# Top-k attention and a low-rank mixer in one kernel: weighted values moved from the middle of a step to the head of the next one

## The chip, the cores and the metric

The kernel runs on one core of a Trainium2 chip. A core has a matrix engine (TensorE, PE in the profile), a vector engine (VectorE, DVE), a scalar engine (ScalarE, ACT), a general-purpose engine (GpSimd, POOL) and a queue that issues transfers (SyncE, SP). Each works through its own queue in order; they wait for each other by semaphores. The time is the device time of the core in microseconds, the median over runs; beside it stands one execution that was recorded instruction by instruction.

## The reference, cut to what matters

Two blocks follow each other. Attention keeps only the 32 largest scores of each row:

```python
# q, k, v: (8, 8, 576, 64)
scores = scale * np.matmul(q, k.transpose(0, 1, 3, 2))
kth = np.partition(scores, -top_k, axis=-1)[..., -top_k:-top_k + 1]
scores = np.where(scores >= kth, scores, -1000000000.0)
attn = np.exp(scores - np.max(scores, axis=-1, keepdims=True))
attn = attn / (np.sum(attn, axis=-1, keepdims=True) + 1e-09)
attn_out = np.matmul(attn, v)
```

The heads are then laid side by side, x of shape (8, 576, 512), and a mixer runs over them:

```python
h = x.transpose(0, 2, 1) @ U @ V          # U: (576, 32), V: (32, 576)
u = x + h.transpose(0, 2, 1)
out = u + np.maximum(u @ w_ch1, 0.0) @ w_ch2   # 512 -> 2048 -> 512
```

## The kernel before, in words

**Tiles and steps.** A pair of heads of one batch is a unit of work `g`; there are 32 (four per batch, `NPAIR`). The 576 rows of a pair are cut into five tiles (`CH`): four of 128 rows for both heads, and a fifth (`t == NT`) with the last 64 rows of both heads in one tile. So there are 160 steps (`STEPS`), and one loop runs over them; tile `m` is pair `m // 5`, tile `m % 5`. The code of a step writes the order of each engine's queue by hand: what is called first stands first in the queue of every engine that it uses. No scheduler changes it.

**The life of a tile.** `scores(n + 1)` is called at the head of step `n`: matmuls of q with k (L322), which work with 64 rows of the array for each head, and ScalarE's copies to `Ssb` (L349, L339 for the fifth tile). `fold` and `split` (GpSimd L387 and L390, VectorE L389) halve the rows for the search. `front`, a generator that the step advances piece by piece, finds the 32nd largest of each row in four rounds on VectorE (L429 to L460), masks the rest (ScalarE L482 and L485, GpSimd L488) and takes the exponential with the row sums (ScalarE L394, `den`). The probabilities are then transposed, because the next product needs them by columns. From tile `ROUNDED` (30) on, the four full tiles of a pair go through VectorE's 32 x 32 transposes (L515) and through memory: four transfers to `away` (L521) and one back into `PT` (L525), all issued by SP in `blocks`. Only their last columns, and the fifth tile, are transposed on TensorE (L543, L548 in `turns`).

**Weighted values.** `values(g, t)` multiplies the transposed probabilities with v into the PSUM tile `O`. For a full tile this is one matmul over the whole array (L577) and eight with 64 columns of the array (L581), four for each head, two of which run side by side. ScalarE copies `O` to `XT` (L590). For the fifth tile it is five matmuls over the whole array (L567); VectorE inverts the pair's row sums (`inverse`, L556) and ScalarE scales the result by them (L575). In the steady part, `values(n - 2)` is called in the middle of step `n`, after five of its eight shares of mixer work.

**Mixing.** When the values of a pair are complete, `mixed` is put on the list `mixing`: TensorE transposes `XT` (L602), ScalarE copies (L606), GpSimd multiplies by the inverted row sums (L607); after five more shares come the product with U (L613), its copy `Tb` (L621), and in two further shares the product with V and the addition of x (L625, L627), copied to `uT` (L635). After the fourth pair of a batch the batch's perceptron `mlp` is put on the list `fillers`.

**Shares.** `fill` is called eight times in a step. Each call advances the generator in front of `mixing` by one piece, and then takes from `fillers` as many of the perceptron's matmuls (L650 for the first layer, L669 for the second) as a share allows, so that a batch's perceptron is spread over the steps of the next batch. If `fillers` is empty, the share is dropped, and its work is left for the end. The second layer's results are copied (ScalarE L684), added to `uT` (GpSimd L685), transposed back (TensorE L717), copied (L719) and written out. The transposition of an output tile is normally issued ten matmuls after the tile's last one, but that of the batch's last tile stands directly behind its own addition.

**Buffers.** The PSUM pool `ps_t`, which has two tiles, serves all transposes, `O` and the mixing; `ps_s`, with two, the scores; `ps_m`, with two, the perceptron. `PT` has two buffers, and v is held in three.

The first batch (`n < ALONE`, 20 steps) runs without perceptron work, with an order of its own, and during it the weights are converted; the change leaves those steps alone.

Of the kernel before, what the change touches and what calls it, by code (L numbers as in the profile page):

```python
# [26 lines left out]
def kernel(  # L27
# [39 lines left out]
    NPAIR = H // 2  # L67
# [165 lines left out]

    raw, qkTs, S2s, uTs, XTs, dens = {}, {}, {}, {}, {}, {}
    probs, PTs, folds, fronts_of = {}, {}, {}, {}

    def load(g):
        b, h0 = g // NPAIR, 2 * (g % NPAIR)
# [313 lines left out]
    def inverse(g, lo, hi):  # L552
        den = dens[g][:, lo:hi]
        if g == NPAIR - 1:
            nc.vector.tensor_scalar_add(den, den, 1e-9)
        nc.vector.reciprocal(den, den)  # L556

    def values(g, t):

        PT = PTs.pop((g, t))  # L560
        va, vd, vt = (a[g % NV] for a in (vas, vds, vts))
        O = ps_t.tile([P, P], F32, tag="tp", name="O")
        if t == NT:
            den, x = dens[g], xs[g % 2]
            inverse(g, 2 * NT if g == NPAIR - 1 else 0, 2 * NT + 1)
            for j in range(NT + 1):
                nc.tensor.matmul(  # L567
                    O,
                    lhsT=PT[:, j],
                    rhs=va[:, :, j, :] if j < NT else vt,  # L570
                    start=(j == 0),
                    stop=(j == NT),
                )
            for h in range(2):
                nc.scalar.mul(x[half(h), NT, half(h)], O[half(h), half(h)], den[half(h), 2 * NT :])  # L575
            return
        nc.tensor.matmul(O, lhsT=vd, rhs=PT[:, 2 * NT], start=True, stop=False)  # L577
        PB = PT[:, 0 : 2 * NT].rearrange("p (a h) (c j) -> p h c a j", h=2, c=NT)
        for j in range(NT):
            for h in range(2):  # L580
                nc.tensor.matmul(  # L581
                    O[half(h)],
                    lhsT=va[:, h, j, :],
                    rhs=PB[:, h, j] if shared(g, t) else PT[:, NT * h + j],
                    start=False,
                    stop=(j == NT - 1),
                )
        if t == 0:
            XTs[g] = attn.tile([P, MAIN], F32, tag="XT", name="XT")
        nc.scalar.copy(XTs[g][:, cols(t)], O)  # L590


    def mixed(g, wait):

        b, gi = divmod(g, NPAIR)
        if gi == 0:
            uTs[b] = mlpp.tile([P, NC, S], F32, tag="uT", name="uT")
        XT, den = XTs.pop(g), dens[g]
        X = xs[g % 2]
        tp = ps_t.tile([P, NT, P], F32, tag="tp", name="tp")  # L600
        for t in range(NT):
            nc.tensor.transpose(tp[:, t, :], XT[:, cols(t)], ident)  # L602
        X4 = X[:, 0:NT, :].rearrange("p t (h d) -> p t h d", h=2)
        tp4 = tp.rearrange("p t (h d) -> p t h d", h=2)
        den4 = den[:, 0 : 2 * NT].rearrange("p (t h) -> p t h ()", h=2).to_broadcast([P, NT, 2, D])
        nc.scalar.copy(X4, tp4)  # L606
        nc.gpsimd.tensor_tensor(X4, X4, den4, ALU.mult)  # L607
        for _ in range(wait):
            yield
        pT = ps_t.tile([P, P], F32, tag="tp", name="pT")  # L610
        for t in range(NT + 1):
            i = t % NT * R
            nc.tensor.matmul(  # L613
                pT[i : i + R, :],
                lhsT=U[:, t, :],
                rhs=X[:, t, :],
                start=(t < NT),
                stop=(0 < t),
            )
        Tb = mlpp.tile([P, P], F32, tag="Tb", name="Tb")  # L620
        nc.scalar.copy(Tb, pT)  # L621
        yield
        for chunks, (lo, hi) in zip(PARTS, SPAN):
            up = ps_t.tile([P, WIDE], F32, tag="tp", name="up")
            nc.tensor.matmul(up[:, 0 : hi - lo], lhsT=Tb, rhs=V[:, lo:hi], start=True, stop=False)  # L625
            for t in chunks:
                nc.tensor.matmul(  # L627
                    up[:, OFF[t] - lo : OFF[t] - lo + rows(t)],
                    lhsT=X[:, t, :],
                    rhs=ident if t < NT else ident2,  # L630
                    is_transpose=True if t < NT else None,
                    start=False,
                    stop=(t == chunks[-1]),
                )
            nc.scalar.copy(uTs[b][:, gi, lo:hi], up[:, 0 : hi - lo])  # L635
            yield
        if gi == NPAIR - 1:
            fillers.append(mlp(b))
# [103 lines left out]
    def fill(k=1):  # L742
# [3 lines left out]
        for _ in range(k):  # L746
# [5 lines left out]
            while due > 0:  # L752
# [6 lines left out]
                else:  # L759
                    due -= done  # L760

    load(0)
    next_params(1)
    t = 0
# [5 lines left out]
    for n in range(STEPS + 2):  # L770
        g, t = divmod(n, CH)
        if n < STEPS:
            if t == 0 and g + 1 < NP:
                load(g + 1)
            if t == 1 and g + 1 < NP:
                ready = prep(g + 1)
            fronts[n] = front(g, t)
            next(fronts[n])
        here, last = fronts.get(n, iter(())), fronts.pop(n - 1, iter(()))
        if n >= ALONE - 1 and n <= ALONE:  # L780

            if n < ALONE:
                next(last)
                values(*divmod(n - 3, CH))
                list(turning)
                next(here)
                next(last)
                scores(*divmod(n + 1, CH))
                fold(*divmod(n + 1, CH))
                values(*divmod(n - 2, CH))  # L790
            list(turns(*divmod(n - 1, CH)))
            values(*divmod(n - 1, CH))
            if n < ALONE:
                split(*divmod(n + 1, CH))
                next(here)
                next(here)
                inverse(g, 0, 2 * NT)
                mixing.append(mixed(g, 1))
                fill()
                next(here)  # L800
                continue
            fill()
            scores(*divmod(n + 1, CH))
            fold(*divmod(n + 1, CH))
            next(here)
            while mixing:
                fill()
            next_params(1)
            fill()
            next(last, None)  # L810
            next(here)
            fill()
            split(*divmod(n + 1, CH))
            next(here)
            next(here)
            fill()
            continue
        ease = eased(*divmod(n - 1, CH))
        if n < ALONE:
            if ease:  # L820
                next(last, None)
            scores(*divmod(n + 1, CH))
            fold(*divmod(n + 1, CH))
            if n >= 3:
                values(*divmod(n - 3, CH))
                if (n - 3) % CH == NT:
                    mixing.append(mixed((n - 3) // CH, 3))
            list(turning)
            fill()
            next(here)  # L830
            if t < NT - 1:
                next_params(1)
            fill()
            next(ready, None)
            next(here)
            next(last, None)
            fill()
            split(*divmod(n + 1, CH))
            next(here)
            if t in (0, 1, NT - 1):  # L840
                next_params(1)
            next(here)
            fill()
            if n >= 1:
                turning = turns(*divmod(n - 1, CH))
            continue
        away = n <= STEPS and shared(*divmod(n - 1, CH))
        if ease:
            next(last, None)
        fill()  # L850
        if n + 1 < STEPS:
            scores(*divmod(n + 1, CH))
            fold(*divmod(n + 1, CH))
        next(turning, None)
        fill()
        next(turning, None)
        if n > ALONE and (n - 1) % CH < NT:
            next(last, None)
        fill()
        next(turning, None)  # L860
        fill()
        if ease:
            next(last, None)
        next(here, None)
        next_params(1)
        fill()
        if n - 2 >= ALONE:
            values(*divmod(n - 2, CH))
            if (n - 2) % CH == NT:
                mixing.append(mixed((n - 2) // CH, 5))  # L870
        next(here, None)
        split(*divmod(n + 1, CH))
        if away:
            blocks(*divmod(n - 1, CH))
        fill()
        if n <= STEPS:
            turning = turns(*divmod(n - 1, CH))
        next(here, None)
        next(ready, None)
        if t in (1, 3):  # L880
            next_params(1)
        next(here, None)
        fill(2)
# [33 lines left out]
```

## Time and profile before

| | |
|---|---|
| median of 3 runs | 1743.06 us (1742.22 to 1745.01) |
| the profiled execution | 1742.03 us, its span from the first to the last instruction 1740.2 us |
| TensorE busy, matmuls | 1634.9 us (94%) |
| VectorE busy | 1494.1 us (86%) |
| ScalarE busy | 1023.9 us (59%) |
| GpSimd busy | 956.7 us (55%) |
| the perceptron's matmuls, L650 and L669 | 539.8 us and 545.1 us busy |
| weighted values, L581 | 145.0 us busy, 2048 records |
| scores, L322 | 209.6 us busy, 1334 records |
| chain that ended last | TensorE 78%, VectorE 11%, DMA 3%, ScalarE 3% |

How to read it: the span is one execution, from the program's first instruction to its last. A row of a group or of the timeline names the line of the kernel, the engine, the operation, the tile written and the tiles read, and the shape; with a matmul, `128*64` means 128 rows and 64 columns of the array. A matmul of 32-bit numbers appears as two records, one for each pass. In a row of the timeline that merges several records, the start is that of the first, and the duration is that until the last one ends; matmuls overlap, so the distance between the starts of two rows says more than the duration. A bracket gives the idle time of the engine before the row and who ended it. In a list of waits stand the total in us, how often, and the longest. In the windows view each engine has busy microseconds and, in brackets, its number of instructions; behind them stand the granted TensorE clock, the share of the DMA engines and GB/s. In a line of 40 slices a digit is the busy share in tenths.

### The profile page before, as it was taken

The numbers are of one execution on the slowest core, as the hardware profiler recorded it, in microseconds if no ns is written. First come the engines' busy times: TensorE is split into PE (matmuls) and PEld (weight loads), VectorE is DVE, ScalarE is ACT, GpSimd is POOL, SyncE is SP. The second block draws the span as 40 slices with busy tenths as digits, with TensorE's granted clock in tenths as the row PEclk, the third lists the DMA queues.
The fourth block names the chain that finished last, engine by engine and source line by source line (L and its number), as shares of the span: only waits on it lengthen the run. The fifth ranks groups of instructions, "written<-read, shape, count | busy, mean of one in ns | idle before, by whom it ended". The sixth has DMA issues, their size and how long they took to land.

```text
span 1740.2 us, 29711 instructions
## 1 busy us (share of the span) xinstructions
PE 1634.9 (94%) x9489; PEld 1208.1 (69%) x9489; DVE 1494.1 (86%) x4358; ACT 1023.9 (59%) x2582; POOL 956.7 (55%) x759
## 2 busy tenths in 40 slices
PE   4566789999999999999999999999999999999999
PEld 2344556777677876778677776687667876687677
DVE  7999889899999999999999999999999999993000
ACT  4888788665655666565656665565656656563100
POOL 4778688656555555555555555556555555552000
PEclk7788899999999999999999999999999999999999
DMA  3332222344434444444444444444444444432010
GB/s 87 91 90 83 73 73 64 78 111 119 119 99 116 117 114 107 112 116 105 118 101 117 114 111 105 112 111 115 110 107 119 114 109 103 117 90 70 4 16 13
DMA packets 275837, 167.37 MB, mean 96 GB/s; under 512 B 173920, under 2 KB 260192, under 8 KB 275680
## 3 DMA queue, kind: packets, MB, share of 16 engines
q1 hardware_dynamic: 274624, 165.20, 36.8%
q8 instruction: 75, 1.23, 0.3%
q14 instruction: 82, 0.67, 0.1%
q10 hardware_dynamic: 1056, 0.26, 0.1%
HBM read 101.42 MB, written 63.96 MB: 95 GB/s over the span
## 4 chain that ended last, share of the span: by engine, by line
PE 78%; DVE 11%; DMA 3%; ACT 3%; POOL 1%; issue 1%; SPq 1%; POOLq 0%; DVEq 0%; ACTq 0%
PE mm L669 27%; PE mm L650 26%; PE sc L322 8%; PE O L581 6%; DVE m L460 4%; DVE hT L455 4%; DMA PT<-away 2%; PE O L567 2%; PE up L625 2%; PE tp L548 1%; DVE first L443 1%; PE O L577 1%; PE tp L543 1%; DMA away<-y 1%; PE up L627 1%
## 5 line engine op out<-in xcount | busy, mean ns | idle before, releaser
L669 PE MATMUL mm<-hT,w 128*128 128x256 f32 (+1 forms) x2048 | 545.1, 411 | 0.0
L650 PE MATMUL mm<-uT,w 128*128 128x256 f32 (+1 forms) x2048 | 539.8, 411 | 0.0
L488 POOL TENSOR_TENSOR Ssb<-Ssb,E 128x576 f32<-128x576 f32 x271 | 378.7, 1415 | 283.5 <-ACT E L485 283.2
L650 PEld LDWEIGHTS mm<-uT,w 128*128 128x128 f32 x2048 | 376.0, 192 | 100.0 <-issue 13.3
L669 PEld LDWEIGHTS mm<-hT,w 128*128 128x128 f32 x2048 | 374.4, 192 | 94.7 <-issue 11.5
L460 DVE MAX8 m<-upper 128x8 f32<-128x304 f32 x756 | 323.7, 465 | 2.9
L390 POOL TENSOR_TENSOR lower<-lower,upper 128x576 uint32<-128x576 uint32 (+1 forms) x140 | 180.2, 1287 | 110.4 <-DVE upper L389 103.3
L394 ACT ACTIVATE Ssb<-Ssb,nmax 128x576 f32<-128x576 f32 x286 | 221.6, 779 | 17.4 <-POOL Ssb L465 9.6
L455 DVE MATCH_REPLACE8 upper<-m,upper 128x304 f32<-128x304 f32 x504 | 227.5, 458 | 0.0
L662 ACT ACTIVATE hT<-mm 128x320 f32<-128x320 f32 (+1 forms) x256 | 104.8, 409 | 203.5 <-PE mm L650 201.8
L387 POOL TENSOR_TENSOR lower<-Ssb 128x576 uint32<-128x576 uint32 (+1 forms) x140 | 181.5, 1296 | 69.5 <-ACT Ssb L349 23.5
L322 PE MATMUL sc<-qkT 64*128 64x288 f32 x1334 | 209.6, 437 | 8.6 <-ACT Ssb L356 7.8
L485 ACT ACTIVATE E<-Ssb,least 128x576 f32<-128x576 f32 x271 | 197.9, 769 | 5.2
L322 PEld LDWEIGHTS sc<-qkT 64*128 64x128 f32 x1334 | 115.4, 182 | 94.5 <-issue 42.6
L349 ACT COPY Ssb<-sc 128x576 f32<-128x576 f32 x216 | 127.1, 640 | 83.4 <-PE sc L322 82.1
L515 DVE STREAM_TRANSPOSE y<-Ssb 128x512 f32<-128x512 f32 x208 | 142.9, 702 | 22.8 <-ACT Ssb L394 20.9
L581 PE MATMUL O<-PT,va 128*64 128x128 f32 x2048 | 145.0, 285 | 8.5 <-DMA PT<-away 8.5
L429 DVE MAX8 upper<-lower 128x8 f32<-128x288 f32 x252 | 103.0, 445 | 38.3 <-POOL lower L390 38.3
L581 PEld LDWEIGHTS O<-PT,va 128*64 128x64 f32 x2048 | 113.5, 141 | 25.5 <-DMA PT<-away 10.8
L682 DVE TENSOR_TENSOR oT<-uT,mm 128x320 f32<-128x320 f32 (+1 forms) x8 | 3.6, 454 | 144.1 <-PE mm L669 144.1
L590 ACT COPY XT<-O 128x128 f32<-128x128 f32 x128 | 34.2, 267 | 143.3 <-PE O L581 143.2
L455 DVE MATCH_REPLACE8 upper<-first,upper 128x304 f32<-128x304 f32 x252 | 114.0, 459 | 0.0
(95 smaller groups left out, 2068.7 us busy)
## 6 DMA issues: line engine op xcount, KB each, us to landing
away<-y SPq DMA_DIRECT2D x416, 128.0 KB, 2.4
PT<-away SPq DMA_DIRECT2D x104, 512.0 KB, 3.3
raw<-in_moe_w_ch_dram SPq DMA_DIRECT2D x32, 512.0 KB, 3.9
va<-in_v_dram SPq DMA_DIRECT2D x64, 128.0 KB, 2.3
out_dram<-ob SPq DMA_DIRECT2D x57, 128.0 KB, 2.0
ld<-in_q_dram SPq DMA_DIRECT2D x108, 64.0 KB, 2.7
ld<-in_k_dram SPq DMA_DIRECT2D x108, 64.0 KB, 2.4
ld<-in_q_dram SPq DMA_DIRECT2D x108, 8.0 KB, 2.3
```

The costliest lines, as they stand in the source:

```text
L322: nc.tensor.matmul(out, lhsT=qkT[half(h), 0, cols(t)], rhs=qkT[half(h), 1, lo:hi], start=True, stop=True,)
L387: nc.gpsimd.tensor_tensor(bottom, a.bitcast(U32), b.bitcast(U32), ALU.add)
L390: nc.gpsimd.tensor_tensor(bottom, bottom, top.bitcast(U32), ALU.subtract)
L394: nc.scalar.activation(E, chunk, AF.Exp, bias=nmax, scale=SCALE, accum_out=total)
L455: nc.vector.match_replace(nxt, ms[c], curs[c], NEG)
L460: nc.vector.max(ms[c], curs[c])
L485: nc.scalar.activation(gap, chunks[c], AF.Relu, bias=least[:, c : c + 1], scale=-WIDEN)
L488: nc.gpsimd.tensor_tensor(chunks[c], chunks[c], gap, ALU.subtract)
L515: nc.vector.transpose(y[:, :, h].rearrange("p r c j -> p c r j"), E2[:, a : a + MAIN].rearrange("p (c r j) -> p c r j", c=NT, r=4),)
L581: nc.tensor.matmul(O[half(h)], lhsT=va[:, h, j, :], rhs=PB[:, h, j] if shared(g, t) else PT[:, NT * h + j], start=False, stop=(j == NT - 1),)
L650: nc.tensor.matmul(ph[:, 0:w], lhsT=w1[:, cc, f * P : (f + 1) * P], rhs=uT[:, cc, lo:hi], start=(cc == 0), stop=(cc == NC - 1),)
L669: nc.tensor.matmul(po[:, 0:w], lhsT=w2[:, f, c * P : (c + 1) * P], rhs=hTs[f][:, 0:w], start=(f == 0), stop=(f == NF - 1),)
```

## The change

The values of tile `n - 3` are now called at the head of step `n`, after its first share and directly before the scores of tile `n + 1`, instead of those of tile `n - 2` in its middle: every tile's values come half a step later. This holds for the tiles from `ALONE` (20) to `STEPS - 3` (157); the last two keep their places in the two steps behind the loop. The inversion of a pair's row sums stays in the middle of the step where the fifth tile's values stood, and so now comes half a step ahead of those values. `mixed` gets a further argument, `lag`: it lets one share go by before its first piece. It is 1 for all pairs but the last.

```diff
+    inverted = set()
...
         if t == NT:
             den, x = dens[g], xs[g % 2]
-            inverse(g, 2 * NT if g == NPAIR - 1 else 0, 2 * NT + 1)
+            if g not in inverted:
+                inverse(g, 2 * NT if g == NPAIR - 1 else 0, 2 * NT + 1)
...
-    def mixed(g, wait):
-
+    def mixed(g, wait, lag=0):
+
+        for _ in range(lag):
+            yield
         b, gi = divmod(g, NPAIR)
...
+    def weighted(m):
+
+        values(*divmod(m, CH))
+        if m % CH == NT:
+            mixing.append(mixed(m // CH, 5, 1 if m < STEPS - 1 else 0))
...
         fill()
+        if ALONE <= n - 3 <= STEPS - 3:
+            weighted(n - 3)
         if n + 1 < STEPS:
             scores(*divmod(n + 1, CH))
             fold(*divmod(n + 1, CH))
...
         fill()
-        if n - 2 >= ALONE:
-            values(*divmod(n - 2, CH))
-            if (n - 2) % CH == NT:
-                mixing.append(mixed((n - 2) // CH, 5))
+        if n >= STEPS:
+            weighted(n - 2)
+        elif n - 2 >= ALONE and (n - 2) % CH == NT:
+            inverted.add((n - 2) // CH)
+            inverse((n - 2) // CH, 0, 2 * NT + 1)
         next(here, None)
         split(*divmod(n + 1, CH))
```

## The prediction

> **What bounds the kernel now.** I read the busy table and the slices first.
>
> ```profile
> PE 1634.9 (94%) x9489; PEld 1208.1 (69%) x9489; DVE 1494.1 (86%) x4358; ACT 1023.9 (59%) x2582; POOL 956.7 (55%) x759
> PE   4566789999999999999999999999999999999999
> DVE  7999889899999999999999999999999999993000
> ```
>
> TensorE is full from slice 8 to the end, VectorE nearly so while there are steps. The windows view says which is first:
>
> ```profile
> 343.70:439.10 95.40, 90.90 (x578) 71.48 (x577) 92.08 (x282) 57.17 (x151) 54.70 (x44) 1.00 0.45 116
> 439.10:1567.00 1127.90, 1124.41 (x6658) 833.02 (x6657) 1069.12 (x3250) 682.17 (x1753) 639.05 (x505) 1.00 0.43 110
> ```
>
> After the length come PE, PEld, DVE, ACT, POOL. From 439 us PE is busy 99.7% and VectorE 94.8%: PE bounds. Before that VectorE (96.5%) is as tight as PE (95.3%).
>
> Busy PE is not PE at its peak, so I read starts in its timeline:
>
> ```profile
> 843.72 0.38 PE L577 MATMUL O<-PT,vd 128*128 128x128 f32 x2
> 844.04 1.09 PE L581 MATMUL O<-PT,va 128*64 128x128 f32 x16
> 845.06 2.96 PE L650 MATMUL mm<-uT,w 128*128 128x320 f32 x10
> 847.95 1.24 PE L322 MATMUL sc<-qkT 64*128 64x288 f32 x8
> 849.12 0.33 PE L548 MATMUL tp<-ident,Ssb 128*128 128x128 f32 x1
> 849.29 3.40 PE L650 MATMUL mm<-uT,w 128*128 128x320 f32 x12
> 852.52 0.38 PE L577 MATMUL O<-PT,vd 128*128 128x128 f32 x2
> 852.84 1.09 PE L581 MATMUL O<-PT,va 128*64 128x128 f32 x16
> 853.86 3.50 PE L650 MATMUL mm<-uT,w 128*128 128x320 f32 x12
> 857.29 1.24 PE L322 MATMUL sc<-qkT 64*128 64x288 f32 x8
> ```
>
> Twelve mixer matmuls between a transpose and the values (849.29 to 852.52) take 3.23 us, 0.269 each. The same twelve between values and scores (853.86 to 857.29) take 3.43. So a stretch that starts after column tiles (128*64) and ends at row tiles (64*128) costs 0.20 us more; single starts put 0.10 at its first weight load and 0.09 at its end.
>
> The one place where column tiles meet scores directly is early, with L613's column tiles:
>
> ```profile
> 207.62 0.41 PE L613 MATMUL pT<-x,U 128*32 128x128 f32 x2 [0.67 <-ACT x L575]
> 207.96 1.24 PE L322 MATMUL sc<-qkT 64*128 64x288 f32 x8
> 209.13 0.81 PE L625 MATMUL up<-V,Tb 128*128 128x320 f32 x2
> ```
>
> From the last L613 start to the scores is 0.20 us, the same as to a full matmul elsewhere, and the scores then take 1.17 us (207.96 to 209.13) as always (847.95 to 849.12). One switch is paid, not two.
>
> Last, the waits, and a transpose of finished output at a batch handover:
>
> ```profile
> PE O L581 <- DMA PT<-away: 8.5, 12, 2.3
> ACT XT L590 <- PE O L581: 143.2, 114, 3.7
> 431.51 0.73 POOL L685 TENSOR_TENSOR oT<-oT,uT 128x256 f32<-128x256 f32 x1
> 432.30 0.44 PE L717 MATMUL tp<-ident,oT 128*128 128x128 f32 x2 [1.63 <-POOL oT L685]
> 631.57 0.44 PE L717 MATMUL tp<-ident,oT 128*128 128x128 f32 x2
> ```
>
> At 432 PE waits 1.63 us for the copy and the addition of the output that it has just made. At 631.57 it waits for nothing: the values (1.43 us from 630.14) lie in between.
>
> **What the skill says.** The Trainium skill, "TensorEngine Tiling (Array Packing)", Key Properties: "Changing tiling mode (not just tile) drains the TensorE". The trace agrees: 0.09 us at each such change. The Trainium skill, "TensorE: Matmul & The Clock Gate", Step-by-step: weight loads are pulled ahead of running matmuls; the trace shows 0.10 us where that fails, at the first weights after column tiles. The same page, Architectural detail: ScalarE and VectorE queues are strictly first in, first out. The 143.2 us in which ScalarE stood before the copy of O agree.
>
> **The change, part by part.**
>
> *Values next to the scores.* The same nine matmuls per tile, moved later by half a step on PE. In the built order values of the four full tiles of each pair stand directly before scores 109 times; tiling changes fall from 632 to 523. By 0.20 us that is 21.8 us of PE time, 18.4 (92 places) after 439 us and 3.4 before. The fifth tile (L567, full array) before scores saves nothing: its change to row tiles is paid as before. Bounds: nothing, if O to scores costs both switches after all; 0.30 a place (32.7), if the drain hides too. I take 0.20, from L613.
>
> *Later values, so the reloaded probabilities are awaited less.* From the starts, L577 to L581 exceeds its usual 0.205 us eleven times between 350 and 1570 us, by 7.0 us; 3.9 of it after 439. The largest excess is 1.2 us; the values now come about 3.5 us later, after seven mixer matmuls. All go. The last wait (2.3 us at 1586) stays, as the last two tiles keep their place, but two transposes and an up-projection now stand before it: −0.9.
>
> *ScalarE and VectorE.* The copy of O (L590, 0.27 us) moves ahead of the copies of the scores, which wait for a later PE instruction anyway: nothing. What was queued behind it in mid-step (Exp, mask) comes free earlier. The reciprocal (L556, 0.2 us) keeps its place. The transposes' buffer PT is reused by a transfer that the step issues after the split, after these values: no wait. SP's issues are unmoved.
>
> *Mixing, five shares later.* POOL's multiply (L607, 1.04 us) now precedes L390 in its queue. VectorE, behind L390, has y and two rounds (over 3 us) between L389 and L429: hidden, 1 us for each of 27 pairs without that cover. Scores no longer lie between L607 and L613; the smallest slack of 3.5 us falls to about 2.
>
> *Handovers.* As mixing ends later, the last L669 chain of five batches (the second to the sixth) is followed at once by its own L717, with the values no longer between. Queued behind it on PE are the next batch's matmuls and scores, so the whole wait counts. The wait of 432 us is what this costs: 1.5 × 5 = 7.5, less 0.1 × 5 for a dearer switch there. The last batch's handover is as before.
>
> *The first handover.* The second batch's mixer is ready 5/8 step later and the first runs dry: by the built order seven matmuls (2 passes × 0.269 each, 3.8 us) fall out of step 41 and are done at the very end. PE meanwhile waits for L607, L685 and Tb one after the other, about 2.7 us more than now. Before 439 us VectorE has only 3.3 us of idle time in 95, so I let that stretch gain 2.5 in all, and the 3.8 come on top at the end.
>
> **Sum.** After 439: −18.4 − 3.9 − 0.9 + 7.5 − 0.5 = −16.2. Before: −2.5 + 3.8 = +1.3. Together −14.9; I take −14, since VectorE goes from 94.8% to 96% busy and some of its waits may reach PE. The profiled execution took 1742.03 us (span 1740.2 and 1.8 around it), 1.0 below the median of 1743.06. From the median: 1729.
>
> **Rivals.**
>
> *VectorE becomes the bound* (0.15). Its 58.8 us of idle after 439 would have to shrink to about 43. If its waits (on L390, L394, L349) were of its own making, only those for L349, 9 us, could go: −9 + 1.3 gives 1735, with small stalls up to 1739. Against: no PE wait for it shows now, and L389 is done 3.8 us before the scores that need its buffer.
>
> *The switch is not saved* (0.07). Then −3.9 − 0.9 + 7.0 + 1.3 = +3.5: 1746; about no change.
>
> *Slower: the handover waits behind POOL's queue* (0.05). If L685 there stands behind L488 twice and L387 (2 × 1.4 + 1.4 = 4.2 us) instead of beside them, each wait grows by 4.2: +21 in five, 1750. It decides once each wait passes 1.5 + 14/5 = 4.3 us. Against: L488 ends about 2 us after the scores' end, when that chain ends too.
>
> *More than forecast* (0.05): handovers hidden, VectorE following: 1720.
>
> **How the numbers follow.** The likeliest case, 0.68, has 1724 to 1735 and gives 1729. The range 1722 to 1739 adds most of the VectorE case and some of the larger gain. A measurement here tells about 0.2% (3.5 us) from no change: faster means under 1739.6. Faster: 0.68 + 0.12 + 0.05 = 0.85; same 0.08; slower 0.07, of it 0.02 for what I have not seen, such as the longer mixer stretch outrunning ScalarE's two PSUM buffers (smallest slack now 1.14 us).
>
> **What would show it.** Right: scores 0.20 us after the last L581; no extra in stretches of mixer matmuls; PE's waits on PT nearly gone but the last; five new waits of L717 on L685 near 1.5 us; the final stretch seven matmuls longer; VectorE near 96%. Wrong: PE waiting for L389, L394 or L662 in most steps, or L581 to scores near 0.30 or more.

## The result, and the profile after

The changed kernel takes 1723.52 us (median of 4 runs, 1722.87 to 1724.09), the kernel before 1744.03 us beside it (1742.22 to 1745.91). The ratio is 0.9882, with a 95% interval of 0.9865 to 0.9899. A later set of runs of the same kernel gave 1723.44 us and 0.989 (0.9873 to 0.9906). The prediction said 1729 us, in a range from 1722 to 1739.

In the changed kernel the lines stand a little lower: the values are L579, L583 and L569 (were L577, L581, L567), the scores L323, the copy to `XT` L592, the reciprocal L557, the scaling of the fifth tile L577, the perceptron L654 and L673, the addition to `oT` L689 and the transposition behind it L721. In the rows, `x22` counts passes, two to a matmul; the prediction's "twelve mixer matmuls" are twelve passes, too.

First the busy table and the slices of the profile after, as they were read before:

```profile
PE 1611.4 (94%) x9489; PEld 1217.8 (71%) x9489; DVE 1487.7 (86%) x4358; ACT 1024.7 (60%) x2582; POOL 958.4 (56%) x759
PE   4566789998999999999999999999999999999999
DVE  7999888999999999999999999999999999992000
```

The number of instructions is the same on every engine. TensorE has 23.5 us less of busy time than before (1634.9), and the span is 19.3 us shorter (1740.2 to 1720.9): the time was taken out of TensorE's own queue, and its idle time grew by 4.2 us. The share (94%) says nothing of that, since both sides of it shrank.

To see where, I cut the span at the same places: at the starts of the scores issued in step 43 (for tile 44) and in step 158 (for tile 159, the last). The windows view after, whose columns are as before, cut at those starts:

```profile
341.30:434.30 93.00, 87.94 (x565) 71.38 (x563) 92.44 (x286) 57.92 (x154) 55.94 (x45) 0.98 0.48 121
434.30:1546.50 1112.20, 1105.88 (x6652) 841.50 (x6650) 1064.79 (x3251) 683.36 (x1751) 642.41 (x506) 1.00 0.44 112
1546.50:1720.90 174.40, 168.34 (x780) 134.29 (x778) 18.91 (x49) 30.55 (x79) 10.38 (x11) 1.00 0.10 24
```

Beside the stretches of before, which the same scores bound, and the terms of the prediction that belong to each:

| stretch | before, us | after, us | difference | predicted |
|---|---|---|---|---|
| start to the scores of tile 44 | 439.1 | 434.3 | −4.8 | −2.5 |
| from there to the scores of tile 159 | 1127.9 | 1112.2 | −15.7 | −18.4 − 3.9 + 7.5 − 0.5 = −15.3 |
| from there to the end | 173.2 | 174.4 | +1.2 | −0.9 + 3.8 = +2.9 |
| span | 1740.2 | 1720.9 | −19.3 | −14.9 |

One full step and the head of the next from TensorE's timeline after:

```profile
846.37 0.38 PE L579 MATMUL O<-PT,vd 128*128 128x128 f32 x2
846.68 1.09 PE L583 MATMUL O<-PT,va 128*64 128x128 f32 x16
847.71 1.24 PE L323 MATMUL sc<-qkT 64*128 64x288 f32 x8
848.88 0.66 PE L544 MATMUL tp<-ident,Ssb 128*128 128x128 f32 x4
849.37 0.70 PE L654 MATMUL mm<-uT,w 128*128 128x320 f32 x2
849.91 0.27 PE L549 MATMUL tp<-ident,Ssb 128*128 128x128 f32 x1
850.02 6.09 PE L654 MATMUL mm<-uT,w 128*128 128x320 f32 x22
855.95 1.05 PE L569 MATMUL O<-va,PT 128*128 128x128 f32 x8
```

The column tiles (`128*64`) are followed at once by the row tiles (`64*128`), and the scores take their usual 1.17 us (847.71 to 848.88). The perceptron's long stretch, 22 passes from 850.02 to 855.95, takes 5.93 us or 0.270 each: nothing is left of the 0.20 us that a stretch between values and scores used to hold.

The waits of TensorE after, over the whole span, of which these two rows answer to those of before (total, times, longest):

```profile
PE tp L721 <- POOL oT L689: 11.0, 7, 3.4
PE O L583 <- DMA PT<-away: 1.0, 1, 1.0
```

The wait for the reloaded probabilities has gone from 8.5 us in twelve places to 1.0 us in one, and the wait for the finished output has grown from 2.9 us in two to 11.0 us in seven. One of the five new ones, from the timeline after:

```profile
1016.49 0.72 POOL L689 TENSOR_TENSOR oT<-oT,uT 128x256 f32<-128x256 f32 x1 [0.21 <-ACT oT L688]
1017.26 0.44 PE L721 MATMUL tp<-ident,oT 128*128 128x128 f32 x2 [1.26 <-POOL oT L689]
```

### The profile page after: what moved, and what is told of

Same layout as the page of the kernel before. It is cut to its first block, busy times and chain, and to the rows that moved or that the text cites. A ratio compares the mean times of both kernels' runs of the same rounds, so it can differ in the third digit from the quotient of the medians.

```text
span 1720.9 us, 29703 instructions
## 1 busy us (share of the span) xinstructions
PE 1611.4 (94%) x9489; PEld 1217.8 (71%) x9489; DVE 1487.7 (86%) x4358; ACT 1024.7 (60%) x2582; POOL 958.4 (56%) x759
## 4 chain that ended last, share of the span: by engine, by line
PE 74%; DVE 18%; POOL 3%; issue 2%; ACT 2%; DMA 1%; SPq 1%; POOLq 0%; DVEq 0%; ACTq 0%
PE mm L654 25%; PE mm L673 25%; PE sc L323 8%; PE O L583 6%; DVE m L461 6%; DVE hT L456 4%; DVE upper L456 2%; DVE first L444 2%; PE O L569 2%; PE tp L549 2%; PE up L629 1%; PE O L579 1%; PE tp L544 1%; PE up L631 1%; PE tp L721 1%
## 5 line engine op out<-in xcount | busy, mean ns | idle before, releaser
L673 PE MATMUL mm<-hT,w 128*128 128x256 f32 (+1 forms) x2048 | 530.9, 407 | 0.0
L654 PE MATMUL mm<-uT,w 128*128 128x256 f32 (+1 forms) x2048 | 522.9, 407 | 1.5 <-ACT hT L666 1.5
L654 PEld LDWEIGHTS mm<-uT,w 128*128 128x128 f32 x2048 | 380.0, 191 | 99.2 <-issue 2.6
L673 PEld LDWEIGHTS mm<-hT,w 128*128 128x128 f32 x2048 | 377.3, 191 | 92.3 <-issue 3.0
L323 PE MATMUL sc<-qkT 64*128 64x288 f32 x1334 | 209.0, 436 | 8.4 <-ACT Ssb L357 7.6
L323 PEld LDWEIGHTS sc<-qkT 64*128 64x128 f32 x1334 | 115.0, 181 | 63.1 <-issue 22.8
L350 ACT COPY Ssb<-sc 128x576 f32<-128x576 f32 x216 | 127.5, 643 | 31.3 <-PE sc L323 30.0
L583 PE MATMUL O<-PT,va 128*64 128x128 f32 x2048 | 143.6, 284 | 1.0 <-DMA PT<-away 1.0
L583 PEld LDWEIGHTS O<-PT,va 128*64 128x64 f32 x2048 | 112.4, 140 | 17.2 <-issue 1.6
L430 DVE MAX8 upper<-lower 128x8 f32<-128x288 f32 x252 | 102.7, 444 | 15.3 <-POOL lower L391 14.6
L483 ACT ACTIVATE least<-m 128x2 f32<-128x2 f32 (+1 forms) x159 | 32.2, 202 | 132.5 <-DVE m L461 131.7
```

The lines of the kernel that those rows point to most:

```text
L323: nc.tensor.matmul(out, lhsT=qkT[half(h), 0, cols(t)], rhs=qkT[half(h), 1, lo:hi], start=True, stop=True,)
L583: nc.tensor.matmul(O[half(h)], lhsT=va[:, h, j, :], rhs=PB[:, h, j] if shared(g, t) else PT[:, NT * h + j], start=False, stop=(j == NT - 1),)
L654: nc.tensor.matmul(ph[:, 0:w], lhsT=w1[:, cc, f * P : (f + 1) * P], rhs=uT[:, cc, lo:hi], start=(cc == 0), stop=(cc == NC - 1),)
L673: nc.tensor.matmul(po[:, 0:w], lhsT=w2[:, f, c * P : (c + 1) * P], rhs=hTs[f][:, 0:w], start=(f == 0), stop=(f == NF - 1),)
```

## The experiments

**The theories.** *Tiling changes*: the gain is that of the prediction, 0.20 us of TensorE time at each place where the values of a full tile now stand directly before the scores (109 places, 92 of them after 439 us); the delay of the values by itself about nets out, since what it saves in waits for the reload it pays at the handovers. *Delay*: the gain is that the values come later, so that reloads, and ScalarE's copies of `O`, no longer hold anything up, and the place next to the scores has nothing to do with it. *Neighbourhood*: the two need only be neighbours, in whichever order.

### The same delay, without the neighbourhood; and the neighbours the other way round

In the first kernel the values of tile `n - 3` stand one share behind the scores:

```diff
-        if ALONE <= n - 3 <= STEPS - 3:
-            weighted(n - 3)
         if n + 1 < STEPS:
...
         fill()
+        if ALONE <= n - 3 <= STEPS - 3:
+            weighted(n - 3)
         next(turning, None)
```

> The changed kernel, but the values of tile n - 3 stand one share behind the scores, between matmuls of the mixer or the next transposes, and not directly before the scores. They are as late as in the changed kernel, within a quarter step, and the array changes its mode 631 times, as before (632), not 523. Theory of the modes (each place where column tiles meet row tiles directly saves 0.20 us): the gain of 109 x 0.197 = 21.5 us is gone, 1743 us (1739 to 1748). Theory of the delay (the gain comes from values that no longer wait for reloaded probabilities, and from ScalarE no longer standing before the copy of O in mid-step): 1723 us, within 3.

In the second they stand directly behind them:

```diff
-        if ALONE <= n - 3 <= STEPS - 3:
-            weighted(n - 3)
         if n + 1 < STEPS:
             scores(*divmod(n + 1, CH))
             fold(*divmod(n + 1, CH))
+        if ALONE <= n - 3 <= STEPS - 3:
+            weighted(n - 3)
         next(turning, None)
```

> The changed kernel, but the values stand directly behind the scores, not directly before them: the same neighbour, the other order, with the full-array matmul (the last rows of v) between row tiles and column tiles. The array changes its mode 632 times. Theory of the modes: no gain from the neighbourhood as such, 1743 us (1739 to 1748). Theory of the delay, or of the neighbourhood whatever the order: 1723 us, within 3.

Measured: 1749.7 us one share behind (ratio 1.0038, 1.0023 to 1.0053) and 1754.57 us directly behind (1.0065, 1.0048 to 1.0081); before took 1742.56 beside them. Both are slower than before, so neither the delay nor the neighbourhood as such holds the gain. Neither of TensorE's lists of waits shows a wait for `PT` between 440 and 1590 us: the delay did what it does, and it was not what counts. But both also lie above the 1739 to 1748 us of the theory of the modes, and the timelines say why. (The sums that follow are of distances between starts on TensorE, from the scores of tile 44 to those of tile 159.) One share behind:

```profile
853.17 0.39 PE L579 MATMUL O<-PT,vd 128*128 128x128 f32 x2
853.49 1.09 PE L583 MATMUL O<-PT,va 128*64 128x128 f32 x16
854.51 6.19 PE L654 MATMUL mm<-uT,w 128*128 128x320 f32 x22
860.63 1.24 PE L323 MATMUL sc<-qkT 64*128 64x288 f32 x8
```

The same 22 passes now take 6.12 us from start to start, 0.19 more than in the kernel after. This is the price of a lost place, and it is there again. Beyond it, column tiles here also come to stand directly before single transposes and up-projections: the up-projections cost 3.6 us more than in the kernel after, and the transposes of the probabilities 4.0. The stretch takes 1133.3 us, 21.1 more; another 3.7 us are lost before it and 2.8 behind it.

Directly behind the scores:

```profile
849.89 1.24 PE L323 MATMUL sc<-qkT 64*128 64x288 f32 x8
851.07 0.49 PE L579 MATMUL O<-PT,vd 128*128 128x128 f32 x2
851.48 1.09 PE L583 MATMUL O<-PT,va 128*64 128x128 f32 x16
```

`values` begins with a matmul over the whole array (L579), so this order has all four changes: to rows, to the whole array, to columns, and back. And the pair L579 takes 0.41 us until L583 starts, where the kernel after has 0.31: at this place the first weights after row tiles cost 0.10 more. The Trainium skill, "TensorE: Matmul & The Clock Gate", Step-by-step, says that weights are pulled ahead where the row groups don't conflict, or where they go to a background buffer; the 0.10 us look like a place where this fails, but no run here shows which condition it was. The stretch takes 1143.4 us, 31.2 more than in the kernel after. Of these 12.2 lie at the first weights of 115 values (92 full tiles and 23 fifth ones), 8.5 at the change to the scores, and most of the rest at the transposes (4.9) and up-projections (2.4) that now follow the values.

### The purest cut: one share between values and scores

The order of values and scores is kept, with only the head's share (a matmul or two, or a product of the mixing) between them. In a second kernel this is done for tiles 0 and 2 of each pair alone (`ahead = (n - 3) % CH in (0, 2)`), so that 55 of the 109 places are lost; a third is the kernel after, once more.

```diff
+        ahead = (n - 3) % CH < NT
+        if ahead and ALONE <= n - 3 <= STEPS - 3:
+            weighted(n - 3)
         fill()
-        if ALONE <= n - 3 <= STEPS - 3:
+        if not ahead and ALONE <= n - 3 <= STEPS - 3:
             weighted(n - 3)
```

> The changed kernel, but the values of the full tiles stand ahead of the head's share and not behind it: the one or two matmuls of the mixer in that share (at times an up-projection) come between values and scores, and nothing else moves. The array changes its mode 632 times, as before the change. Theory of the modes: each of the 109 places costs 0.197 us again, all that lies after 439 us (92) on the path, those before it hidden by VectorE: 1723.5 + 18 = 1741.5 us (1739 to 1745). If the neighbourhood is incidental: 1723.5 within 2.

> The same for the first and third tile of each pair alone: 54 places keep values directly before scores, 55 lose it, 578 changes of mode. Theory of the modes: half of the difference of the kernel with all places, 1723.5 + 9 = 1732.5 us (1730 to 1735).

> The changed kernel once more, beside the two others on the same chip: 1723.5 us within 1.5.

Measured on the same chip: 1741.52 us with all places lost (ratio 0.9996, 0.9987 to 1.0004), 1730.71 us with half of them lost (0.9933, 0.9914 to 0.9952), 1723.44 us for the kernel after (0.989, 0.9873 to 0.9906), before 1742.16. The timeline of the first:

```profile
872.72 0.38 PE L579 MATMUL O<-PT,vd 128*128 128x128 f32 x2
873.03 1.09 PE L583 MATMUL O<-PT,va 128*64 128x128 f32 x16
874.06 0.81 PE L629 MATMUL up<-V,Tb 128*128 128x320 f32 x2
874.70 0.55 PE L631 MATMUL up<-ident,x 128*128 128x128 f32 x4
```

The 0.10 us of unhidden weights is visible in the row behind the column tiles: the two passes of L629 take 0.64 us until the next row starts, in the kernel after 0.54 (1010.27 to 1010.81).

So the whole gain hangs on nothing being between values and scores: one share in between gives all of it back. 1741.52 − 1723.44 = 18.1 us; at the scores of tile 44 both kernels are at 434.4 and 434.3 us, so it falls on the 92 places after that, 0.197 us each. This is the price of two changes where one would do. The half version loses 7.3 us in all. From the scores of tile 44 to those of tile 159 it takes 1121.4 us, 9.2 more than the kernel after, which is 0.20 for each of the 46 places that it loses there; it had reached the scores of tile 44 1.5 us sooner, at 432.8, where other things than these places set the time. All three kernels met their expectations. The delay, which is the same in all three up to a share, nets to 0.6 us against before, which is within what can be told from nothing.

### Does the early inversion matter?

The prediction costed the reciprocal at nothing because it keeps its place. The change could also have let it go along with the values. Without the branch, `values` of the fifth tile inverts by itself, at the head of the step:

```diff
         if n >= STEPS:
             weighted(n - 2)
-        elif n - 2 >= ALONE and (n - 2) % CH == NT:
-            inverted.add((n - 2) // CH)
-            inverse((n - 2) // CH, 0, 2 * NT + 1)
         next(here, None)
```

> The changed kernel, but the reciprocal of the row sums stands with the fifth tile's values again, so on VectorE it comes half a step later, at the head of the step; ScalarE's scaling of the values waits for it, ahead of the copies of the scores. If TensorE bounds and VectorE follows with microseconds to spare: no difference, 1723.5 us within 2. If ScalarE's wait reaches the scores and from there VectorE in each of 27 pairs by 0.5 us or more: 1735 or above.

Measured: 1752.02 us (ratio 1.0054, 1.0037 to 1.0072): 28.5 us more than the kernel after, and slower than before (1741.53 beside it). The first of the two cases named falls; the time is that of the second, above 1735, but its path is another one. In the list of ScalarE's waits of this kernel, from 440 to 1570 us, there is a row that the kernel after doesn't have:

```profile
ACT x L577 <- DVE den L557: 61.7, 23, 3.0
```

and its timeline (the scores, with VectorE's and ScalarE's rows at one such place) shows what stands in front:

```profile
1022.61 1.24 PE L323 MATMUL sc<-qkT 64*128 64x288 f32 x8
1022.67 0.81 DVE L434 MAX8 upper<-lower 128x8 f32<-128x288 f32 x2
1023.39 0.83 DVE L444 MAX8 first<-upper 128x8 f32<-128x304 f32 x2
1024.15 0.20 DVE L557 RECIPROCAL den<-den 128x9 f32<-128x9 f32 x1
1024.44 0.63 ACT L577 ACTIVATE x<-O,den 64x64 f32<-64x64 f32 x2 [2.80 <-DVE den L557]
1025.09 1.18 ACT L350 COPY Ssb<-sc 128x576 f32<-128x576 f32 x2
```

The same place in the kernel after:

```profile
1001.48 1.24 PE L323 MATMUL sc<-qkT 64*128 64x288 f32 x8
1001.59 0.63 ACT L577 ACTIVATE x<-O,den 64x64 f32<-64x64 f32 x2 [1.08 <-PE O L569]
1002.28 1.18 ACT L350 COPY Ssb<-sc 128x576 f32<-128x576 f32 x2
```

The reciprocal takes 0.2 us, but it stands behind a search round in VectorE's queue. ScalarE's scaling waits for it, and behind that the copies of the new scores, which start 2.48 us after the scores instead of 0.80. The Trainium skill, "TensorE: Matmul & The Clock Gate", Architectural detail, calls both queues strictly first in, first out; these rows agree. TensorE in turn waits for the scaling, which by the code frees the PSUM tile that the next transposes take (`PE tp L606 <- ACT x L577`, 11.9 us in 17 places from 440 to 1570 us). By the starts of the scores of the recorded executions, 11.5 us of the loss lie before tile 44 and 18.0 between tiles 44 and 159, 0.78 for each of 23 pairs. Of these 18.0 TensorE loses 16.2 from start to start directly before L606. The late copies of the scores are not what counts: VectorE's waits for them (`DVE upper L390 <- ACT Ssb L350`) are 9.6 us in either kernel from 440 to 1570 us. That the inversion comes half a step ahead is therefore not an aside: without it the move loses.

### The handovers

Two edits at the five new waits. The first takes out the lag, so that the mixing ends a share sooner:

```diff
-            mixing.append(mixed(m // CH, 5, 1 if m < STEPS - 1 else 0))
+            mixing.append(mixed(m // CH, 5))
```

> The changed kernel without the share by which mixing begins later (lag 0 for all pairs). At the batch handovers values and scores then lie again between the last output tile and its transposition. If the wait there is what I read it as (1.43 us in five places, 3.4 at the first): 1715 us (1712 to 1718). If the lag is needed, because the transposes of XT then stand directly behind the transpose of the probabilities and wait for ScalarE's copies in 27 pairs by 0.3 us or more: 1723 or above.

In the second, the batch's last output tile is transposed among the next batch's work, after the sixteen matmuls of the first four chains of its first layer: the list `late` of tiles not yet transposed is made once for the kernel and no longer in each batch's `mlp`.

```diff
         uT = uTs.pop(b)
-        late = []
...
-        late.pop()()
+        if b == B - 1:
+            late.pop()()
...
     fillers, mixing, due = [], [], 0.0
+    late = []
```

> The changed kernel, but the transposition of a batch's last output tile is left to the next batch's perceptron (it is issued there after the fourth chain of the first layer), so nothing stands directly behind its own addition but the very last tile. If TensorE bounds everywhere and these waits are pure loss: 5 x 1.43 + 3.4 + 1.3 = 11.9 us less, 1712 us (1709 to 1715). If VectorE is the next bound right behind TensorE, part of it comes back as other waits: 1716 to 1722.

A third kernel has both edits.

> The moved transposition of a batch's last output tile, and mixing without the lag, on the changed kernel. The lag costs nothing any more once nothing stands behind its own addition: 1713 us within 2. If mixing a share earlier is worth something of its own, at the first handover: 1711.

| | us | ratio to before |
|---|---|---|
| no lag | 1719.43 (1718.87 to 1720.07) | 0.9865 (0.985 to 0.9879) |
| last tile later | 1713.16 (1712.99 to 1713.99) | 0.983 (0.9815 to 0.9844) |
| both | 1713.54 (1712.11 to 1714.17) | 0.9838 (0.9816 to 0.9859) |

Without the lag the waits for L689 from 440 to 1570 us shrink from 6.3 to 1.7 us in the same five places:

```profile
PE tp L721 <- POOL oT L689: 1.7, 5, 0.3
```

With the last tile later they are gone, as the timeline of that kernel shows at the batch border that was shown of the kernel after:

```profile
1011.71 0.60 PE L672 MATMUL mm<-hT,w 128*128 128x256 f32 x2
1012.15 6.09 PE L653 MATMUL mm<-uT,w 128*128 128x320 f32 x22
1018.07 0.38 PE L579 MATMUL O<-PT,vd 128*128 128x128 f32 x2
...
1020.74 2.86 PE L653 MATMUL mm<-uT,w 128*128 128x320 f32 x10
1023.44 0.38 PE L721 MATMUL tp<-ident,oT 128*128 128x128 f32 x2
```

The second layer's last matmuls (L672 here) are followed at once by the next batch's first ones, and L721 comes 11.7 us later without a wait. The gain is 10.4 us against the kernel after (1723.52), in the range that was expected. By the starts of the scores, 1.8 us of the difference are there by tile 44, 6.4 come in the stretch with the five handovers, and 1.7 behind the scores of tile 159. With it the lag makes no difference (0.4 us, within the ranges); without it, taking the lag out gained 4 of the 8 us that were expected. In the stretch with the five handovers it gains 4.2, as 0.3 us of waiting are left at each; at the end 1.7; but it comes to the scores of tile 44 2.3 us later, and there the transpositions of `XT` find ScalarE not yet done (`PE tp L606 <- ACT x L577`, 1.4 us in two places from 300 us on). The version with the last tile later beats both kernels: 1713.16 us, 29 us under before (1742.56 beside it).

### The first handover

The prediction counted the batch that runs dry before the second batch's perceptron as a loss. `EARLY` scales the shares up to step 42; at 0.87 instead of 0.91 the first batch's work lasts over that place, to after the scores of tile 44. (By the count of the code it is step 42 that runs dry, between the scores of tiles 43 and 44; the prediction and the first of the expectations say step 41.)

```diff
-    SLOTS, SHORT, EARLY = 8, 0.65, 0.91
+    SLOTS, SHORT, EARLY = 8, 0.65, 0.87
```

> The changed kernel with the early shares at 0.87 instead of 0.91 of a full one: ten matmuls of the first perceptron move from steps 20 to 40 into step 41, which runs dry in the changed kernel; from step 42 on both orders have done the same work. If step 41's waits are pure loss, and the steps before it are bound by VectorE anyway: 3 us less, 1720.5 (1719 to 1722). If TensorE bounds already before step 41 and its waits there are work that VectorE needs anyway: 1723.5 within 1.

> The early shares at 0.87 and the last output tile of a batch left to the next perceptron, on the changed kernel. If the waits add up: 1713.2 - 1 to 2 = 1711.5 us (1710 to 1713), as 3.4 us of the first handover are already gone with the moved transposition and only the waits for the mixing are left there.

Measured: 1725.62 us on the kernel after (1725.51 to 1728.07; ratio 0.9909, 0.989 to 0.9928) and 1714.92 us on the version with the last tile later (1714.59 to 1715.56; 0.9845, 0.9827 to 0.9863). Neither brings the gain that was expected, and both are about 2 us slower than the kernels they start from. That they are slower is not shown: they ran on another chip, and the intervals of the ratios overlap. The timeline of the kernel after, around its first handover, and a row of its windows view:

```profile
428.40 0.44 PE L721 MATMUL tp<-ident,oT 128*128 128x128 f32 x2 [3.37 <-POOL oT L689]
...
430.32 1.44 PE L629 MATMUL up<-V,Tb 128*128 128x320 f32 x2 [0.92 <-ACT Tb L625]
...
434.34 1.20 PE L323 MATMUL sc<-qkT 64*64 64x288 f32 x10
...
428.30:434.30 6.00, 4.97 (x36) 3.69 (x36) 6.00 (x18) 3.13 (x9) 2.14 (x3) 0.72 0.54 143
```

and with `EARLY` at 0.87:

```profile
434.76 1.20 PE L323 MATMUL sc<-qkT 64*64 64x288 f32 x10
...
439.50 0.69 PE L721 MATMUL tp<-ident,oT 128*128 128x128 f32 x2 [1.79 <-POOL oT L689]
439.98 7.37 PE L654 MATMUL mm<-uT,w 128*128 128x320 f32 x22
...
439.50:447.20 7.70, 7.70 (x25) 5.41 (x26) 4.36 (x13) 2.86 (x8) 0.79 (x1) 0.80 0.17 44
```

The kernel after waits 4.3 us there, the other 1.2 (from 415 us to these scores), and both reach the scores of tile 44 within 0.5 us of each other: VectorE sets their time. In the first windows row of the profile after it is busy 92.44 of 93.00 us, and in the row here 6.00 of 6.00. What TensorE loses in that stretch is covered. Moved behind it, the handover falls where TensorE is busy for 7.70 of 7.70 us and VectorE for 4.36, and it also costs more than its wait: the 22 passes after it take 7.21 us instead of 5.93. In the kernel that also has the last tile later no such wait is left at this handover. It loses nothing behind the scores of tile 44. It comes to them 1.8 us later; at earlier scores the two kernels lie up to 1.8 us apart either way, so this alone tells little.

## Why the prediction was right

The main terms were right in kind and size. The saving was still larger than forecast: 20.5 us against the kernel before beside it, where 14 were expected, so the time lies near the lower end of the range and 0.5 us under the 1724 to 1735 of the likeliest case.

**The saved tiling changes** (−21.8 in all, −18.4 of them counted after 439 us). Right in kind, place and size. The distance from L583 to the scores is 0.20 us, the mixer stretches hold no extra 0.20, and the cut with one share between puts it at 0.197 us a place after the scores of tile 44. That the whole middle stretch came out within 0.4 us of its sum is partly luck: TensorE also had 12 passes of 320 columns more and 18 of 256 fewer there, 0.7 us less in all, which the sum does not contain.

**Waits for the reload** (−3.9). As said: none is left but the last.

**Handovers** (+7.5 and −0.5). Five new waits of 1.3 us idle each, 1.43 over the usual distance from start to start, so 7.2 instead of 7.5. The mechanism is shown from the other side too: with the last tile's transposition moved away from its own addition they are gone.

**Before 439 us** (−2.5, measured −4.8). This term was mis-sized, and its reasoning was half right: that VectorE bounds there was said, but the text then charged TensorE's 2.7 us of extra waiting against the gain. With VectorE busy 92.44 of 93.00 us this waiting is covered, and so is the saving from fewer tiling changes: the kernel with one share between values and scores, which has none, reaches the scores of tile 44 at 434.4 us all the same, and the one with the values directly behind the scores at 433.5. (With the values one share behind it is 438.0, but that kernel waits 4.8 us for the mixing's `Tb` and `x` between 340 and 440 us.) So what was gained there goes with the delay. One trace of it is in VectorE's waits for ScalarE from 215 us to these scores: 3.4 us before (for the exponential, L394, 2.3 and for the copies of the scores, L349, 1.1), none after. That fits a ScalarE that no longer stands before the copy of `O`; no run took it apart from the reload.

**The end** (+2.9, measured +1.2). Seven matmuls of 320 columns (3.8 us) were to come on top, less 0.9 at the last wait for `PT`. What came on top is nine of 256 columns, 3.9 us. The wait fell by 1.3, from 2.27 to 0.99 us, and with it went something that the text had not counted. TensorE's timeline of before at that place:

```profile
1585.83 0.38 PE L577 MATMUL O<-PT,vd 128*128 128x128 f32 x2
1588.48 1.09 PE L581 MATMUL O<-PT,va 128*64 128x128 f32 x16 [2.27 <-DMA PT<-away]
1589.51 5.41 PE L669 MATMUL mm<-hT,w 128*128 128x256 f32 x16
1594.75 0.60 PE L543 MATMUL tp<-ident,Ssb 128*128 128x128 f32 x4
```

The sixteen passes from 1589.51 to 1594.75 take 5.24 us. At 0.216 each, as elsewhere, they would take 3.46. After the change the wait is shorter and what follows runs at its usual pace: another 1.8 us, of which the text knew nothing. So the term was mis-sized at the wait, not at the work.

**VectorE** (0.9 of margin for it). It went from 94.8% to 95.7% busy after the scores of tile 44, near the 96% named, and no wait of TensorE for it came up: the margin was not needed.

**The inversion** (nothing, as its place is kept). Right for the change as it is. The text did not see that keeping it there is what the rest stands on; the experiment without it showed 28.5 us.

The early stretch, the end and the margin make 4.9 of the 5.5 us between 1729.0 and 1723.5.

Of the rivals, that the switch is not saved is excluded by the 0.20 us (the kernel with one share between is that case, and takes 1741.5 where 1746 was named, for the same two terms); a handover behind GpSimd's queue is excluded by waits of 1.3 us instead of over 4; VectorE as the bound holds only before the scores of tile 44, where it hid a loss and a saving alike.

## What to carry to other kernels

Where matmuls of different array tilings alternate, try to put them directly next to each other in the order that needs the fewest changes, without even a small filler matmul in between: here 18 of 1742 us hung on that. Look at distances between starts; TensorE's busy share was 94% before and after and showed nothing of it. When work is moved in hand-written queues, ask for each small operation that it drags along what it will stand behind in its own queue, and leave it behind if another engine waits for it. A stall is worth taking out only where its engine sets the time; one that another engine covers is best left where it is.

## What the runs showed of the hardware that was not expected

The price at a tiling change has two parts that show up apart. A change itself is about 0.09 us (in the kernel before, from the mixer's last pass to the scores 0.309 us, where to the next pass it is 0.216; medians at 256 columns), and the first weights behind column or row tiles are another 0.10 (L579 to L583 0.41 us instead of 0.31 behind row tiles; L629 0.64 instead of 0.54 behind column tiles).

A wait of TensorE can cost more than itself, because the granted clock falls after it. The windows view of before, at the last reload:

```profile
1586.00:1588.40 2.40, 0.21 (x2) 0.02 (x1) 0.00 (x0) 0.00 (x0) 0.72 (x1) 1.00 0.82 251
...
1590.00:1593.00 3.00, 3.00 (x8) 2.38 (x8) 0.00 (x0) 0.00 (x0) 0.00 (x0) 0.50 0.00 0
```

The clock (third column from the end) is 1.00 during the wait and 0.50 in the 3 us from 1590 on; in the trace it stays there for 3.4 us. That is 1.8 us lost in matmuls after a wait of 2.27. The Trainium skill, "TensorE: Matmul & The Clock Gate", Part 1, says that an idle window of about 3.4 us on a free-running clock leads to half clock. Here less than a whole idle window was enough: a wait of 2.27 us in one place and one of 1.79 us in another (a mean of 0.80 from 439.5 to 447.2 us with `EARLY` at 0.87). The 3.37 us at the first handover of the kernel after left a mark as well (0.72 from 428.3 to 434.3), the handover waits of 1.3 us after 500 us none.
